# Turning batch 0's q and k in 64x64 pieces straight from their landed rows, with a new order on all engines

## The chip, the cores and the metric

The kernel runs on one core of a Trainium2 chip. The metric is the time of one execution in microseconds (us); lower is better. The kernel before took 135.5 us (the median of three runs, 134.92 to 135.55).

A core has engines that run side by side, each through its own list of instructions in order: PE (TensorE, matrix products and transposes, which write to PSUM), ACT (ScalarE) and DVE (VectorE), which work on SBUF and PSUM, POOL (GpSimd) and SP (SyncE), which here mostly issue DMA transfers. An engine that reaches an instruction whose inputs are not there waits, and all that stands behind it on that engine waits too.

## The reference

Two parts run one after the other, on 8 batches of 576 positions.

```python
# attention: q, k, v are (8 batches, 8 heads, 576, 64) in float32
scores = q @ k.transpose / 8 + bias       # bias = -slope[head] * |i - j|
mask   = (i - j >= 0) & (i - j < 128)     # each row sees itself and 127 before it
attn   = softmax(where(mask, scores, -1e9))
x      = (attn @ v), heads side by side   # (8, 576, 512)
# token mixing: w_q, w_k are (512, 64), w_out is (512, 512)
W      = (x @ w_q) @ (x @ w_k).T / 8      # (576, 576) for each batch
out    = relu(W @ x) @ w_out              # (8, 576, 512) in float32
```

As (x w_q) (x w_k)^T x is the same as (x w_q) ((x w_k)^T x), the kernel forms the small product G = (x w_k)^T x, 64 by 512, and never the 576 by 576 one.

## The kernel before, in words

The work is cut into some 730 named operations, each on one engine. Their order is written out by hand in `ORDER` (lines 35 to 118): one word for each, `name@engine`, for PE with `:bank` (the pair of PSUM banks, or one bank of it) and `+n`, which puts n filler matmuls (128x512, on a tile of zeros, `keep_busy`, line 299) ahead of the operation on PE. Each engine runs its words in this order. There is no planner in the kernel itself; semaphores follow from the data.

The stages of a batch b, with names as in `ORDER`:

- **Loads.** `Lq`, `Lk`, `Lv` fetch blocks n of 128 positions, 8 heads, and convert float32 to float16 on the way; `Lt` and `Lv b.4` fetch the last 64 positions of two batches together. All of them are issued by POOL (line 382), each as 128 KB that lands in SBUF. `Lw`, `Lwo` fetch the weights.
- **Turning.** `TQ` (and `TT` for the last 64 positions) transposes q and k on PE with an identity, `ETQ` and `ETT` copy the result from PSUM to `qkT` on ACT or DVE ("evict" it).
- **Scores.** `QK b.g.u`: scores of key block g, heads 4u to 4u+3. `EXP b.g.u` on ACT (line 555) takes the exponential; `MUL b.g` on DVE (line 565) multiplies by the exponential of bias and mask, which lies ready in `bias`, and in `biasl` for the last block.
- **Attention times v.** `PV` on PE; `R` and `X` on DVE divide by the row sums (line 619).
- **Token mixing.** `XT`, `EXT` turn x; `WQ`, `EWQ` and `WK`, `EWK` are the two projections; `G`, `EG` the small product; `MX` and `RM` the product with it and the relu; `OUT`, `EO`, `DO` the last projection, its eviction, and its transfer to memory. The `DO` of batches 0 to 5 stand on POOL behind all loads, those of 6 and 7 on SP.

Batch 0 starts differently, so that the first scores come early (`add_first`, line 390, and `add_tq0`, line 456). Its first 512 positions are loaded by heads: `Lf1.0` (k) and `Lf0.0` (q) fetch heads 0 to 3 as float32, issued by SP; `Lh0.1` (q) and `Lh1.1` (k) fetch heads 4 to 7 as float16, issued by POOL. Each partition p gets positions 4p to 4p+3 of four heads, head by head, in the tiles `nat2` and `nat3`, which batches 2 and 3 use later. Six operations `C` (line 409) then copy these rows into the tile of batch 0, with the four positions outermost and the heads inside, in float16: four with a cast (two each for k and q of heads 0 to 3; one on ACT, three on DVE), two without (heads 4 to 7, DVE). From there each `TQ0.u.j` (u: half of the heads, j: 0 for q, 1 for k) makes 16 transposes: 64 partitions by 128 columns (two heads side by side), so that a product fills all 128 output partitions. Two `ETQ0` for each `TQ0` evict it to `qkT0`, putting the positions back in order.

POOL builds the float32 identity `ident32` (`ident`); `idh` on DVE makes its float16 copy `identh`. `iota`, `dist`, `mask`, `bias0`, `bias1` make the bias tables, and `biasl0`, `biasl1` (line 353, two copies each) rearrange them for the last block. `zeros`, `empty`, `ones`, `pads`, `wqq` set constants and pads.

`cp` (line 234) is a plain copy on the engine named; `cpw` (line 240) is the same, but on ACT it copies pairs of float16 as one float32.

Of the kernel before, what the change touches and what calls it, by code (L numbers as in the profile page):

```python
# [50 lines left out]
EXP1.0.0@ACT WQ0.1@PE:30 Lq2.3@POOL EWK0@DVE EXP1.0.1@ACT XT1.2@PE:20 MUL1.1@DVE G0@PE:31 Lk2.2@POOL
EXT1.2@ACT TQ2.0@PE:0 EG0@ACT MUL1.0@DVE EWQ0.1@ACT Lt2.1@POOL PV1.3@PE:1 ETQ2.0@ACT MX0.0@PE:2
Lt2.0@POOL R1.3@DVE PV1.2@PE:3 RM0.0@ACT X1.3@DVE PV1.0@PE:0 Lwo3@POOL R1.2@DVE R1.0@DVE QK2.0.1@PE:1
X1.2@DVE Lwo0@POOL PV1.1@PE:2 EXP2.0.1@ACT X1.0@DVE Lwo2@POOL QK2.0.0@PE:3 Lwo1@POOL R1.1@DVE
EXP2.0.0@ACT MX0.1@PE:0 X1.1@DVE XT1.1@PE:1 Lk3.2@POOL RM0.1@DVE EXT1.1@ACT XT1.0@PE:2 TQ2.2@PE:3
Lk3.3@POOL EXT1.0@ACT WQ1.1@PE:10 ETQ2.2@ACT MUL2.0@DVE Lq3.2@POOL WK1@PE:11 QK2.1.0@PE:2 Lq3.3@POOL
EWK1@ACT MX0.4@PE:0 QK2.1.1@PE:3 EXP2.1.0@ACT RM0.4@DVE G1@PE:11 EWQ1.1@DVE Lq3.0@POOL TT2@PE:0
EXP2.1.1@ACT EG1@DVE QK2.2.0@PE:2 ETT2@DVE Lq3.1@POOL WQ1.0@PE:10 ETT3@ACT OUT0.2@PE:11 EWQ1.0@DVE
EXP2.2.0@ACT Lk3.1@POOL MUL2.1@DVE QK2.2.1@PE:3 EO0.2@ACT MX1.0@PE:0 Lv2.0@POOL QK2.3.1@PE:2
EXP2.2.1@ACT RM1.0@DVE OUT0.3@PE:10 Lk3.0@POOL EXP2.3.1@ACT OUT0.0@PE:11 MUL2.2@DVE Lv2.1@POOL  # L60
# [837 lines left out]
```

## Time and profile before

| | |
|---|---|
| time, median of 3 runs | 135.5 us (134.92 to 135.55) |
| the profiled execution's own time | 134.75 us |
| its span in the trace | 132.5 us |
| busy, of the span | PE 121.4 us, DVE 114.3, ACT 110.0, POOL 109.5 |
| moved by DMA | 25.12 MB, 190 GB/s in the mean |

The span runs from the first to the last instruction; 2.25 us of the execution's time lie around it. L12 is line 12 of the kernel; many operations go through helpers, so that all transposes show as L232, all other matmuls as L229, plain copies as L238 (DVE) and L236 (ACT), wide ones as L244 (DVE) and L242 (ACT). In a row of a timeline stand the start in us, the time it took (for several instructions, from the first start to the last end), the engine, line and operation, output and input, and the number of instructions; brackets give the engine's idle time before and what ended it. The chain of waits is the work that ended last, followed back from the end, at each step to what released it. In a table of stages each engine has its busy time and its instructions in brackets. Rows of DMA issues give the transfer, its size, and the time from issue to landing. PEld is the load of a matmul's stationary operand.

### The profile page before, as it was taken

Reading aid. Unit: us, or ns where it says so; the run is one execution under the profiler, and the core shown is the slowest. Engines: PE = TensorE matmul, PEld = TensorE weight load, DVE = VectorE, ACT = ScalarE, POOL = GpSimd, SP = SyncE. Lnnn points to the kernel's source line nnn. Section 1 sums busy time; section 2 is a strip of 40 time slices with the busy share of each in tenths; the row PEclk is TensorE's granted clock in tenths of the full one; section 3 lists DMA queues with packets and bytes.
Section 4 is the critical chain, followed back from the end, with each engine's and each line's share of the span. In section 5 each row is a group of like instructions: output and inputs, shape, how many; then the busy total and the mean of one; then the engine's idle time right before and its main releaser. Section 6 shows DMA issues by size and latency. Waiting matters only on the chain.

```text
span 132.5 us, 5417 instructions
## 1 busy us (share of the span) xinstructions
PE 121.4 (92%) x2346; PEld 77.8 (59%) x2346; DVE 114.3 (86%) x191; ACT 110.0 (83%) x161; POOL 109.5 (83%) x147
## 2 busy tenths in 40 slices
PE   6977798899889999999999999999999999999950
PEld 2324466667664577868567576677566756864520
DVE  6899799899959899999899999999899799975730
ACT  5728899999979899999899999999899889563330
POOL 7999979999799999999999999999977960980000
PEclk9999999999999999999999999999999999999996
DMA  3999999999999999999999999999999997598683
GB/s 113 291 159 153 157 153 160 152 143 143 175 159 151 153 154 153 155 149 154 157 153 154 158 149 155 154 157 153 155 172 397 396 378 238 148 308 331 241 306 96
DMA packets 110663, 25.12 MB, mean 190 GB/s; under 512 B 104816, under 2 KB 107888, under 8 KB 110640
## 3 DMA queue, kind: packets, MB, share of 16 engines
q0 software_dynamic: 108128, 21.37, 179.4%
q1 hardware_dynamic: 2512, 3.41, 7.5%
q8 instruction: 18, 0.29, 0.9%
q14 instruction: 5, 0.04, 0.1%
HBM read 29.62 MB, written 9.44 MB: 295 GB/s over the span
## 4 chain that ended last, share of the span: by engine, by line
PE 73%; DVE 15%; ACT 5%; issue 3%; POOL 0%; DVEq 0%; POOLq 0%; ACTq 0%
PE pair L229 63%; PE pair L232 10%; DVE pt L565 4%; ACT pt L555 3%; DVE nat L238 2%; DVE x L619 2%; DVE qkT L244 1%; DVE biasl L244 1%; DVE qkT L238 1%; ACT qkT L242 1%; DVE vtl L330 1%; DVE osb L238 0%; ACT qkT L236 0%; ACT osb L236 0%; DVE wint L317 0%
## 5 line engine op out<-in xcount | busy, mean ns | idle before, releaser
L555 ACT ACTIVATE pt<-pair 128x1024 f16<-128x1024 f32 x64 | 63.7, 1043 | 2.0 <-PE pair L229 1.6
L382 POOL DMA_DIRECT2D vt<-in_v_dram x32 | 32.4, 1136 | 0.0
L229 PE MATMUL pair<-wout_sb,rm 128*128 128x512 f16 (+1 forms) x132 | 32.1, 374 | 0.0
L382 POOL DMA_DIRECT2D nat<-in_q_dram x29 | 29.7, 1052 | 0.6 <-issue 0.5
L382 POOL DMA_DIRECT2D nat<-in_k_dram x29 | 28.7, 1056 | 0.3 <-DMA nat<-in_q_dram 0.3
L565 DVE TENSOR_TENSOR pt<-pt,bias 128x2048 f16<-128x2048 f16 x24 | 28.8, 1217 | 0.1
L229 PE MATMUL pair<-qkT 64*128 64x256 f16 (+2 forms) x320 | 23.4, 250 | 1.6 <-DVE qkT L244 0.7
L619 DVE TENSOR_TENSOR x<-pair,inv 128x512 f16<-128x512 f32 x32 | 21.7, 687 | 1.0
L229 PEld LDWEIGHTS <-pt 128*128 128x128 f16 (+1 forms) x576 | 18.4, 100 | 4.8 <-issue 2.3
L229 PE MATMUL pair<-vt,pt 128*128 128x65 f16 (+1 forms) x512 | 20.9, 194 | 0.0
L236 ACT COPY osb<-pair 128x512 f32<-128x512 f32 (+1 forms) x24 | 14.0, 594 | 5.7 <-PE pair L229 5.5
L229 PEld LDWEIGHTS <-rm 128*128 128x128 f16 x132 | 11.1, 97 | 11.1 <-issue 1.7
L229 PEld LDWEIGHTS <-qkT 64*128 64x128 f16 x320 | 11.4, 94 | 8.8 <-issue 3.9
L804 POOL DMA_DIRECT2D out_dram<-osb x24 | 13.6, 616 | 3.1 <-DVE osb L238 1.0
L232 PE MATMUL pair<-identh,nat 64*128 64x64 f16 x512 | 11.1, 192 | 1.6 <-DVE nat L238 0.9
L232 PEld LDWEIGHTS <-nat 64*128 64x128 f16 x512 | 9.3, 96 | 5.1 <-issue 1.6
L229 PE MATMUL pair<-fill 128*128 128x512 f16 x30 | 10.3, 478 | 1.8 <-DVE fill L362 1.2
L229 PE MATMUL pair<-xT,wqq_sb 128*128 128x256 f16 (+1 forms) x64 | 10.5, 287 | 0.2 <-ACT pt L555 0.2
L740 DVE TENSOR_SCALAR rm<-pair 128x1024 f16<-128x1024 f32 (+1 forms) x9 | 8.8, 983 | 1.8 <-PE pair L229 1.3
L242 ACT COPY qkT<-pair 128x1024 f32<-128x1024 f32 (+1 forms) x11 | 10.0, 907 | 0.2 <-PE pair L232 0.2
L738 ACT ACTIVATE rm<-pair 128x1024 f16<-128x1024 f32 x9 | 9.3, 1049 | 0.5 <-PE pair L229 0.5
L565 DVE TENSOR_TENSOR pt<-pt,biasl 128x2048 f16<-128x2048 f16 x8 | 9.7, 1215 | 0.0
(66 smaller groups left out, 168.1 us busy)
## 6 DMA issues: line engine op xcount, KB each, us to landing
out_dram<-osb POOLq DMA_DIRECT2D x24, 256.0 KB, 5.0
vt<-in_v_dram POOLq DMA_DIRECT2D x32, 128.0 KB, 5.8
nat<-in_q_dram POOLq DMA_DIRECT2D x28, 128.0 KB, 5.6
nat<-in_k_dram POOLq DMA_DIRECT2D x28, 128.0 KB, 5.7
out_dram<-osb SPq DMA_DIRECT2D x7, 256.0 KB, 2.1
out_dram<-osb POOLq DMA_DIRECT2D x6, 128.0 KB, 3.9
nat<-in_k_dram SPq DMA_DIRECT2D x1, 512.0 KB, 3.8
nat<-in_q_dram SPq DMA_DIRECT2D x1, 512.0 KB, 4.8
```

The costliest lines, as they stand in the source:

```text
L229: hold(nc.tensor.matmul(*a, **k))
L232: hold(nc.tensor.transpose(*a))
L236: hold(nc.scalar.copy(out_ap, in_ap))
L238: hold(nc.vector.tensor_copy(out=out_ap, in_=in_ap))
L242: hold(nc.scalar.copy(out_ap.bitcast(FP32), in_ap.bitcast(FP32)))
L382: op = add(kind, b, part, (eng,), deps, lambda o: q.dma_start(out=dst, in_=src), size=size)
L555: nc.scalar.activation(out=pt[:, u, 0:1024], in_=two(s.bank).rearrange("p e c -> p (e c)"), func=AF.Exp, scale=SCALE)
L565: nc.vector.tensor_tensor(out=pt[:, :, 0:1024], in0=pt[:, :, 0:1024], in1=bt, op=ALU.mult)
L619: nc.vector.tensor_tensor(out=x.rearrange("p (g h d) -> p g h d", g=2, h=4), in0=px(slice(0, 64)), in1=box["inv"].unsqueeze(3).broadcast_t ...
L738: hold(nc.scalar.activation(out=out_ap, in_=in_ap, func=AF.Relu, scale=WSCALE))
L740: hold(nc.vector.tensor_scalar(out=out_ap, in0=in_ap, scalar1=0.0, scalar2=WSCALE, op0=ALU.max, op1=ALU.mult))
L804: q.dma_start(out=out[b, P * st:P * st + P, c], in_=osb)
```

## The change

The `C` operations go. `first` now returns the landed rows themselves, in their own layout and type (float32 for heads 0 to 3, float16 for 4 to 7). `TQ0` turns pieces of 64 partitions by 64 columns, one head and one position of the four at a time: 32 pieces where there were 16. A piece of the upper or lower 64 partitions (`h`) of an even or odd head (`e`) goes to the PSUM bank h, partitions 64e to 64e+63. The float16 pieces are transposes with `identh`; the float32 ones are plain float32 matmuls with `ident32`, whose result is float32 in PSUM, so `ETQ0.0` casts to float16 as it evicts; `TQ0.0` needs `ident` and no longer `idh`. The loads `Lq2`, `Lk2`, `Lq3`, `Lk3` now wait for the `TQ0` that reads the tile they overwrite.

`ORDER` is new for all engines. Besides moves within an engine, 67 operations change between ACT and DVE, among them both `biasl`, `ETQ0.0.0.1`, `ETQ0.1.0.1`, `ETT1` (to ACT) and `ETQ0.0.1.1`, `ETQ0.1.1.1`, `EXT0.0` (to DVE). The fillers go from 30 to 22: 8 ahead of the first `TQ0` (10 before) and none ahead of the second (5 before). On DVE, `zeros` and `empty` now stand ahead of `dist` and `mask`, and `wqq` ahead of the first `ETQ0`. The loads of POOL are the same ones in a somewhat different order. The diff shows the start of both orders.

```diff
--- before.py
+++ after.py
@@ -33,88 +33,87 @@
 
 
 ORDER = """
-iota@POOL Lf1.0@SP pads@POOL Lf0.0@SP dist@DVE mask@DVE ident@POOL zeros@DVE bias0@ACT Lw0@POOL
-empty@DVE Lh1.1@POOL bias1@ACT ones@DVE idh@DVE Lh0.1@POOL Lt0.0@POOL C1.0.1@DVE C1.0.0@ACT biasl0@DVE
-Lt0.1@POOL TQ0.0.1@PE:0+10 biasl1@DVE ETQ0.0.1.1@ACT Lq1.3@POOL C0.0.0@DVE C0.0.1@DVE ETQ0.0.1.0@DVE
-Lk1.2@POOL TQ0.0.0@PE:1+5 ETQ0.0.0.0@ACT ETQ0.0.0.1@DVE Lk1.3@POOL QK0.0.0@PE:2+2 C1.1.0@DVE
-QK0.2.0@PE:3 EXP0.0.0@ACT QK0.1.0@PE:0 Lq1.2@POOL TQ0.1.1@PE:1 EXP0.2.0@ACT Lv0.1@POOL C0.1.0@DVE
-ETQ0.1.1.0@DVE TQ0.1.0@PE:2+1 Lv0.0@POOL ETQ0.1.1.1@ACT ETQ0.1.0.1@DVE EXP0.1.0@ACT ETQ0.1.0.0@DVE
-Lq1.0@POOL QK0.2.1@PE:3+3 QK0.1.1@PE:1 Lk1.1@POOL TT0@PE:0 EXP0.1.1@ACT QK0.0.1@PE:2 ETT0@DVE ETT1@DVE
-Lv0.2@POOL EXP0.0.1@ACT MUL0.1@DVE QK0.3.1@PE:1 Lk1.0@POOL EXP0.2.1@ACT MUL0.0@DVE Lq1.1@POOL
-EXP0.3.1@ACT TQ1.2@PE:0+7 Lv0.3@POOL MUL0.2@DVE QK0.3.0@PE:2 ETQ1.2@ACT PV0.0@PE:3 Lv1.3@POOL PV0.1@PE:1
-R0.0@DVE EXP0.3.0@ACT X0.0@DVE QK1.3.1@PE:0 Lv0.4@POOL R0.1@DVE QK1.2.1@PE:3 X0.1@DVE EXP1.3.1@ACT
-Lk2.1@POOL MUL0.3@DVE XT0.0@PE:2+1 QK1.3.0@PE:1 Lw1@POOL EXT0.0@ACT PV0.2@PE:0 Lk2.0@POOL EXP1.3.0@ACT
-QK1.2.0@PE:2 R0.2@DVE X0.2@DVE Lq2.1@POOL EXP1.2.1@ACT TQ1.0@PE:1 MUL1.3@DVE Lv1.2@POOL ETQ1.0@ACT
...
+pads@POOL Lf1.0@SP zeros@DVE iota@POOL empty@DVE Lf0.0@SP ident@POOL dist@DVE mask@DVE Lw0@POOL ones@DVE
+bias0@ACT Lh0.1@POOL bias1@ACT Lh1.1@POOL Lt0.0@POOL TQ0.0.1@PE:0+8 biasl1@ACT Lq1.3@POOL Lq1.2@POOL
+TQ0.0.0@PE:1 wqq@DVE Lt0.1@POOL ETQ0.0.1.0@DVE ETQ0.0.0.0@ACT Lk1.2@POOL ETQ0.0.0.1@ACT ETQ0.0.1.1@DVE
+QK0.0.0@PE:2+3 Lk1.3@POOL EXP0.0.0@ACT QK0.1.0@PE:3 idh@DVE TQ0.1.0@PE:1 Lv0.0@POOL biasl0@ACT
+TQ0.1.1@PE:0 ETQ0.1.0.0@DVE EXP0.1.0@ACT Lv0.1@POOL ETQ0.1.1.0@DVE ETQ0.1.0.1@ACT ETQ0.1.1.1@DVE
+QK0.0.1@PE:2+3 Lv0.2@POOL QK0.1.1@PE:3 EXP0.0.1@ACT QK0.2.0@PE:1 QK0.2.1@PE:0 Lq1.1@POOL EXP0.2.0@ACT
+MUL0.0@DVE Lq1.0@POOL EXP0.1.1@ACT TT0@PE:2+5 Lk1.1@POOL EXP0.2.1@ACT ETT0@DVE MUL0.1@DVE Lk1.0@POOL
+QK0.3.0@PE:1+1 ETT1@ACT EXP0.3.0@ACT TQ1.2@PE:3+1 Lv0.3@POOL MUL0.2@DVE QK0.3.1@PE:0 ETQ1.2@ACT
+PV0.1@PE:2 Lk2.1@POOL PV0.0@PE:1 EXP0.3.1@ACT R0.1@DVE QK1.3.0@PE:3 Lv0.4@POOL R0.0@DVE X0.0@DVE
+EXP1.3.0@ACT Lv1.3@POOL QK1.2.0@PE:0 X0.1@DVE QK1.3.1@PE:1 MUL0.3@DVE EXP1.3.1@ACT QK1.2.1@PE:2
+Lk2.0@POOL PV0.2@PE:3 Lq2.0@POOL R0.2@DVE EXP1.2.0@ACT X0.2@DVE TQ1.0@PE:1+1 Lq2.1@POOL MUL1.3@DVE
+XT0.0@PE:3 ETQ1.0@ACT PV0.3@PE:0 Lw1@POOL EXT0.0@DVE Lv1.2@POOL EXP1.2.1@ACT QK1.0.1@PE:1 R0.3@DVE
+QK1.1.0@PE:3 X0.3@DVE Lv1.0@POOL EXP1.1.0@ACT QK1.0.0@PE:2 MUL1.2@DVE XT0.1@PE:0 Lv1.1@POOL EXP1.0.0@ACT
...
@@ -283,7 +282,6 @@
             tc.add_to_no_dep_group(f"{group(op)}{op.eng}", i)
 
     columns = {
-        "C": lambda op: f"nat{op.batch}",
         "ETQ": lambda op: f"qkT{op.batch}",
         "ETT": lambda op: f"qkT{op.batch}",
         "QK": lambda op: f"qkT{op.batch}",
@@ -395,22 +393,14 @@
         if u == 0:
             raw = raw.bitcast(FP32)
             f = load("Lf", j, u, ("f", 512, 1024), [], raw.rearrange("p (h c) -> p h c", h=4), src, "SP")
-            parts = ((0, 2), (2, 4))
         else:
             raw = raw[:, 0:1024]
             f = load("Lh", j, u, ("c", 512, 1024), [], raw.rearrange("p (h c) -> p h c", h=4), src)
-            parts = ((0, 4),)
-        loads[0, j, u] = []
-        for i, (t0, t1) in enumerate(parts):
-            def cv(o, t0=t0, t1=t1):
-                (cpw if u else cp)(o.eng, first(j, u)[:, t0:t1],
-                                   raw.rearrange("p (h t d) -> p t h d", h=4, t=4)[:, t0:t1])
-
-            loads[0, j, u].append(add("C", j, f"{u}.{i}", EV, [f], cv))
+        loads[0, j, u] = [f]
 
     def first(j, u):
-        return nat_s[0][j].rearrange("p n h d -> p (n h d)").rearrange(
-            "p (u t h d) -> p u t h d", u=2, t=4, h=4)[:, u]
+        raw = nat_s[2 + u][j].rearrange("p n h d -> p (n h d)")
+        return (raw[:, 0:1024] if u else raw.bitcast(FP32)).rearrange("p (h t d) -> p h t d", h=4, t=4)
 
     def add_loads(b):
         pr = b // 2
@@ -421,7 +411,7 @@
         else:
             for n in range(4):
                 for j, t in enumerate((q, k)):
-                    loads[b, j, n] = load("L" + "qk"[j], b, n, ("c", 1024, 256), [tq.get((b - NNAT, j, n))],
+                    loads[b, j, n] = load("L" + "qk"[j], b, n, ("c", 1024, 256), [tq.get((b - NNAT, j, n)), *([tq[0, j, 2 * b - 4]] if b in (2, 3) else [])],
                                           nat_s[b % NNAT][j][:, n],
                                           t[b, :, P * n:P * n + P, :].transpose([1, 0, 2]))
         for t in range(4):
@@ -453,21 +443,29 @@
         r = slice(64 * h, 64 * h + 64)
         tp(out_ap, in_ap, identh[r, r])
 
+    def turned(bank, u):
+        return (two(bank).bitcast(F16)[:, :, 0:512] if u else two(bank)).rearrange("p h (a q) -> p h a q", q=64)
+
     def add_tq0(u, j):
         def em(o):
             for c in range(2):
                 for t in range(4):
-                    for h in range(2):
-                        src = first(j, u)[64 * h:64 * h + 64, t, 2 * c:2 * c + 2, :].rearrange("p a b -> p (a b)")
-                        flip(halves(o.bank, 8, 1)[:, h, 4 * c + t, 0, :], src, h)
-
-        t = add("TQ", 0, f"{u}.{j}", PE, [*loads[0, j, u], idh], em, banks=2, mode=1)
+                    for e in range(2):
+                        for h in range(2):
+                            r = slice(64 * h, 64 * h + 64)
+                            dst = turned(o.bank, u)[64 * e:64 * e + 64, h, 4 * c + t, :]
+                            if u:
+                                tp(dst, first(j, u)[r, 2 * c + e, t, :], identh[r, r])
+                            else:
+                                mm(dst, first(j, u)[r, 2 * c + e, t, :], ident32[r, r], start=True, stop=True)
+
+        t = add("TQ", 0, f"{u}.{j}", PE, [*loads[0, j, u], idh if u else ident], em, banks=2, mode=3)
         for n in (2 * u, 2 * u + 1):
             tq[0, j, n] = t
         for h in range(2):
             def ev(o, h=h):
                 dst = qkT_s[0][:, j, 2 * u:2 * u + 2, 256 * h:256 * h + 256].rearrange("p c (q t) -> p c q t", t=4)
-                src = halves(t.bank, 8, 1)[:, h, :, 0, :].rearrange("p (c t) q -> p c q t", c=2)
+                src = turned(t.bank, u)[:, h].rearrange("p (c t) q -> p c q t", c=2)
                 cp(o.eng, dst, src)
 
             evt[0, j, u, h] = add("ETQ", 0, f"{u}.{j}.{h}", EV, [t], ev, frees=[t], half=h, size=0)
```

More of the change, by code (lines that the diff above doesn't have):

```diff
@@ L51 @@
[L51 to L60, printed above, removed]
-OUT0.1@PE:00 EO0.0@ACT Lv3.3@POOL EO0.3@DVE MX1.4@PE:3 QK2.3.0@PE:2 EO0.1@ACT Lv2.2@POOL RM1.4@DVE
-TQ3.2@PE:1 EXP2.3.0@ACT MX1.1@PE:3 ETQ3.2@DVE OUT1.1@PE:01 Lv2.3@POOL RM1.1@ACT OUT1.4@PE:00 Lk4.0@POOL
@@ new lines @@
+EXP1.1.1@ACT MUL1.0@DVE XT1.2@PE:01 XT0.2@PE:30 Lk2.2@POOL TQ2.0@PE:1 EXT0.2@ACT EWQ0.0@ACT EXT1.2@DVE
+WK0@PE:31 ETQ2.0@ACT MUL1.1@DVE Lk2.3@POOL PV1.3@PE:2 Lwo0@POOL QK2.0.1@PE:0 R1.3@DVE PV1.0@PE:1
+X1.3@DVE EXP2.0.1@ACT Lt2.0@POOL WQ0.1@PE:30 R1.0@DVE PV1.1@PE:2 X1.0@DVE Lwo1@POOL EWK0@ACT EWQ0.1@ACT
+QK2.0.0@PE:0 Lwo2@POOL R1.1@DVE PV1.2@PE:1 X1.1@DVE EXP2.0.0@ACT Lwo3@POOL G0@PE:31 R1.2@DVE Lt2.1@POOL
+X1.2@DVE XT1.0@PE:2 EG0@ACT Lq3.3@POOL EXT1.0@DVE MX0.4@PE:0 MX0.1@PE:1 RM0.4@ACT XT1.1@PE:3 RM0.1@ACT
@@ new lines @@
+MX0.0@PE:2 Lq3.2@POOL EXT1.1@DVE TQ2.2@PE:0 RM0.0@DVE WQ1.0@PE:30 ETQ2.2@ACT Lk3.2@POOL WK1@PE:31
+Lk3.3@POOL QK2.2.1@PE:1 EWK1@DVE QK2.2.0@PE:2 EXP2.2.1@ACT QK2.1.1@PE:0 EWQ1.0@DVE Lk3.0@POOL G1@PE:31
+MUL2.0@DVE EXP2.1.1@ACT WQ1.1@PE:30 Lv2.0@POOL EG1@DVE OUT0.2@PE:10 EXP2.2.0@ACT EWQ1.1@DVE Lq3.1@POOL
+MX1.1@PE:0 EO0.2@ACT QK2.1.0@PE:3 Lk3.1@POOL RM1.1@DVE TT2@PE:2 OUT0.0@PE:11 ETT3@ACT ETT2@ACT
+Lq3.0@POOL EXP2.1.0@ACT MUL2.2@DVE QK2.3.0@PE:2 MX1.4@PE:0 Lv2.1@POOL OUT0.1@PE:10 EXP2.3.0@ACT
@@ L118 @@
+OUT7.1@PE:00 EO7.2@ACT DO7.2@SP OUT7.4@PE:01 EO7.1@DVE DO7.1@SP EO7.4@ACT DO7.4@SP
 """
```

115 lines of the change are left out of this document (57 added, 58 removed).

## The prediction

> **What bounds the kernel now.** I read the busy times of the page first (they stand in the table above; no engine is far ahead of the others), then a table of four stages, then the chain of waits at the start, then single loads against the operations that use them.
>
> ```profile
> 10.50:28.40 17.90, 15.14 (x352) 10.21 (x349) 15.94 (x27) 17.36 (x21) 16.90 (x21) 1.00 2.37 154
> 28.40:66.40 38.00, 36.80 (x797) 25.11 (x796) 34.78 (x56) 35.02 (x49) 36.86 (x45) 1.00 2.28 154
> 66.40:102.00 35.60, 35.52 (x759) 23.37 (x754) 34.02 (x53) 34.82 (x50) 33.93 (x43) 1.00 2.35 174
> 102.00:128.00 26.00, 25.84 (x400) 15.91 (x395) 20.82 (x39) 16.80 (x32) 12.00 (x23) 1.00 0.83 292
> ```
>
> The columns after the length are PE, PEld, DVE, ACT and POOL. From 10.5 to 28.4 ACT is the full engine (17.36 of 17.90 us) and PE has 2.8 us free. From 28.4 on PE is the full one: 1.2 us free up to 66.4, 0.1 up to 102, 0.2 up to 128. ACT keeps 3.0 us free in the second stage and 0.8 in the third. So nothing after 66.4 can be won by a change at the start unless everything arrives there earlier.
>
> What holds ACT back at the start is in the chain of waits:
>
> ```profile
> 5.19 0.45 DVE nat L238
> 5.64 1.69 DVE biasl L244 x4
> 7.33 1.70 DVE nat L238 x2
> ...
> 9.46 0.59 ACT qkT L236
> ...
> 10.10 0.41 PE pair L229 x4
> ...
> 10.53 1.03 ACT pt L555
> ```
>
> DVE casts half of k, copies `biasl`, casts q (`C0.0.0`, `C0.0.1`); only then can `TQ0.0.0` turn q, ACT evict it, `QK0.0.0` run, and ACT's stream of exponentials begin at 10.53.
>
> Second, the loads, which POOL issues one behind the other:
>
> ```profile
> 15.61 1.02 POOL L382 DMA_DIRECT2D vt<-in_v_dram  x1
> vt<-in_v_dram POOLq DMA_DIRECT2D x1, 128.0 KB, 7.5
> 23.07 0.69 PE L229 MATMUL pair<-vt,pt 128*128 128x65 f16 x16
> 28.62 0.92 POOL L382 DMA_DIRECT2D nat<-in_k_dram  x1
> nat<-in_k_dram POOLq DMA_DIRECT2D x1, 128.0 KB, 6.0
> 34.57 0.66 PE L232 MATMUL pair<-identh,nat 64*128 64x64 f16 x32
> 75.87 1.26 POOL L382 DMA_DIRECT2D nat<-in_k_dram  x1
> nat<-in_k_dram POOLq DMA_DIRECT2D x1, 128.0 KB, 5.8
> 82.39 0.63 PE L232 MATMUL pair<-identh,nat 64*128 64x64 f16 x32
> 18.24 0.82 POOL L382 DMA_DIRECT2D vtl<-in_v_dram  x1 [0.73 <-DMA vt<-in_v_dram]
> ```
>
> The load issued at 15.61 lands 7.5 us later, at 23.1, and `PV0.3` uses it at 23.07: no slack. The one at 28.62 lands at 34.6, and `TQ2.2` starts at 34.57: no slack. The one at 75.87 lands at 81.7 and `TQ6.0` starts at 82.39: 0.7 us. In the new order the last load that `PV0.3` needs is still the 17th of POOL's loads, and that of `TQ2.2` the 31st, as before. So the loads are a second bound, which the change moves only as far as POOL's own idle time shrinks (0.73 us in the last row, where POOL waits for an earlier load to land).
>
> **The change part by part.** The durations are of the profiled execution, 134.75 us, of which 132.5 are span.
>
> Removed: the six `C`, and `biasl` from DVE.
>
> ```profile
> 10.13 1.51 DVE L244 COPY nat<-nat 128x1024 f16<-128x1024 f16 x2
> L242 ACT COPY xT<-pair 128x512 f32<-128x512 f32 x7 | 4.1, 590 | 0.5 <-PE pair L232 0.5
> L242 ACT COPY xT<-pair 128x128 f32<-128x128 f32 x5 | 1.3, 268 | 0.2 <-PE pair L232 0.2
> L242 ACT COPY qkT<-pair 128x256 f32<-128x256 f32 x2 | 0.8, 375 | 0.2 <-PE pair L232 0.2
> ```
>
> DVE loses 0.45 + 1.70 + 1.51 us of `C` and 1.69 of `biasl`, 5.4 in all, most of it on the path to 10.53. ACT loses one cast, ahead of that path, and gets `biasl`: per half a copy of 384 float32 and one of 128; between the rows for 512 (0.59) and 128 (0.27) the first is 0.48, so 0.75 per half. `biasl1` stands ahead of the first eviction, `biasl0` behind the first exponential.
>
> The new turning, `TQ0.0`:
>
> ```profile
> 1.25 0.50 SPq L382 DMA_DIRECT2D nat<-in_q_dram  x1
> nat<-in_k_dram SPq DMA_DIRECT2D x1, 512.0 KB, 3.8
> nat<-in_q_dram SPq DMA_DIRECT2D x1, 512.0 KB, 4.8
> 1.19 4.45 PE L229 MATMUL pair<-fill 128*128 128x512 f16 x10 [1.19 <-DVE fill L362]
> 5.77 0.61 PE L232 MATMUL pair<-identh,nat 64*128 64x64 f16 x16
> 6.31 1.63 PE L229 MATMUL pair<-fill 128*128 128x512 f16 x5
> 17.24 0.64 PE L232 MATMUL pair<-identh,nat 64*128 64x64 f16 x32
> 0.74 0.45 SPq L382 DMA_DIRECT2D nat<-in_k_dram  x1
> ```
>
> k lands at 0.74 + 3.8 = 4.55, q at 1.25 + 4.8 = 6.05. Ten fillers take 4.45 us, so eight end near 4.6, and `TQ0.0.1` can start at 4.65 instead of 5.77. Sixteen transposes take 0.61 us there, of which about 0.24 is the latency of the last: eight pairs (the two halves of the partitions run side by side) at 0.049 us a pair. At 17.24 thirty-two take 0.64, less 0.19 for the last: 0.029 a pair, since PE is faster by then; the five fillers from 6.31 take 1.63, between the slow and the fast step, so the turn lies near 7.1.
>
> No float32 matmul is in the trace. Lower end: four pieces at a time (their output halves differ as well) at the pair's price: 8 x 0.049 = 0.4 us for an operation. Upper end: each piece alone with its whole latency: 32 x 0.24 = 7.6. I take 1.6: 16 pairs at 0.049, twice that for twice the bytes of each element; it stays near the row of the same shape. By it `TQ0.0.1` runs from 4.65 to 6.2, and `TQ0.0.0` starts there (q landed at 6.05), does 57% until 7.1 and the rest at the fast price (0.93 x 0.43 = 0.4): 7.5, with the last latency 7.7. What the section TensorE Precision Notes of the page FP8 and Floating Point Precision in the Trainium skill says, that true float32 takes four passes through the array, would with pairs give 3.1 an operation instead of 1.6, and the first exponential at 10.75; no run here shows it. TensorEngine Tiling (Trainium skill, section Tile-to-Partition Mapping) has four independent 64x64 tiles, which would bring that back to 1.6; its section Restrictions adds that column tiling switches the fast weight load off, which speaks against the change.
>
> Evictions from float32: ACT's 0.59 for 512 float32 is the same as the 0.59 for float16 in the chain, so nothing. ACT evicts both halves of q (7.7 to 8.3, 8.9) while `QK0.0.0` runs (0.41), and `EXP0.0.0` starts at **8.9 instead of 10.53: 1.6 us earlier**. Ahead of it on ACT are the bias tables, which come later now:
>
> ```profile
> 2.61 0.55 DVE L334 MEMSET qkT<- 128x256 uint32 x2
> 3.42 0.94 DVE L330 MEMSET vtl<- 64x1056 uint32 x1 [0.26 <-issue]
> 2.65 2.56 ACT L348 ACTIVATE bias<-wint 128x256 f16<-128x256 f32 x8 [0.63 <-DVE wint L317]
> ```
>
> `zeros` and `empty` (1.49) go ahead of `mask`, so the tables run from 4.15 to 6.7 and `biasl1` to 7.45. That hides behind `TQ0.0.0` with 0.25 us to spare; if PE were faster it would cost that. On DVE `wqq` waits for `Lw0` ahead of the first evictions of k; those must be done by 8.3 and have 2 us from 6.2.
>
> What ACT does with the 1.6 us. Before, seven exponentials and one eviction filled 10.53 to 17.92 (`ETQ1.2`):
>
> ```profile
> 17.92 1.01 ACT L242 COPY qkT<-pair 128x1024 f32<-128x1024 f32 x1
> 15.27 2.36 DVE L565 TENSOR_TENSOR pt<-pt,bias 128x2048 f16<-128x2048 f16 x2
> 3.70 0.78 POOL L382 DMA_DIRECT2D nat<-in_q_dram  x1
> nat<-in_q_dram POOLq DMA_DIRECT2D x1, 256.0 KB, 6.0
> ```
>
> Now the same seven and one stand there with `biasl0` (0.75) and `ETT1` (0.38): 8.9 + 7.39 + 1.13 = 17.4, half a microsecond ahead; `EXT0.0` then leaves ACT for DVE (0.59), so 1.1 ahead. DVE gains more: heads 4 to 7 land by 3.70 + 6.0 = 9.7, are turned by 10.4 and evicted by 11.1 to 11.8, and the first `MUL` can start when ACT has done `EXP0.0.1`, near 13.4 instead of 15.27.
>
> The eight fillers fewer (0.22 each) and the longer `TQ0.1` (32 pieces, 0.5 to 1.0 us for 0.41) lie where PE has 2.8 us free: nothing. The loads that now wait for `TQ0` stand on POOL at the place of the load issued at 18.24 and behind it, 10 us after `TQ0.0` ends: nothing.
>
> The sum: 1.1 us on ACT and 1.9 on DVE by 18 us. Then the loads of `PV0.3` and `TQ2.2`, with no slack, stop PE at the same places. If the stream of loads does not move, an earlier ACT and DVE can only fill PE's 1.2 us of idle time between 28.4 and 66.4; if it moves by POOL's 0.73, that much gets through at these two places and the rest has to come from PE's idle time; at `TQ6.0` there are 0.7 us of slack. I take **0.8**, two thirds of PE's 1.2 and about as much as the slack at `TQ6.0`: 134.75 - 0.8 = 133.95 for an execution like the profiled one. The median of the three runs is 0.75 above that execution, so 134.7 for the median.
>
> **The rivals.**
>
> - *The loads swallow it.* `TQ2.2` waits for the same 31st load, POOL's idle time stays, and PE's idle time behind it belongs to other waits. For it: two zero slacks. Against it: ACT and DVE are both ahead. Gain 0 to 0.4: 135.3.
> - *The float32 pieces cost twice what I take, 3.1 us an operation on slow PE.* Then `TQ0.0.1` does 2.45 / 3.1 of its work by 7.1 and ends at 7.5, `TQ0.0.0` at 9.55, and the first exponential starts at 10.75, 0.2 late; DVE is still ahead by what `biasl` and `C` took, so no more than 0.1 comes of it: 135.4. For it: no operation here works on pieces that are halves both ways, so that four at once is not shown. Against it: pairs overlap in every row of transposes. This is the time by the four passes of the Trainium skill's page FP8 and Floating Point Precision (TensorE Precision Notes) without the four tiles of its page TensorEngine Tiling.
> - *Slower: they cost more than that.* The 3.1 us are the point from which it decides. At 6.2 (one piece at a time, and 16 pairs' worth twice over) `TQ0.0.1` ends at 9.3, `TQ0.0.0` at 13.2, and the first exponential starts at 14.4, 3.9 us late, on an engine that is 97% busy until 28.4. Of the 3.9, ACT's 3.0 us of idle time between 28.4 and 66.4 may give back 2.0: 134.75 + 1.9 = 136.65, or 137.4 for the median. For it: the upper end of 7.6 lies beyond it. Against it: again the pairs.
> - *The new order brings waits of its own.* 67 operations change between ACT and DVE; one wait on PE behind a late ACT in stages where PE has 0.1 us free is paid in full. A price of one eviction or exponential (0.6 to 1.0): 136.3. Against it: DVE, 34.0 of 35.6 us busy from 66.4 on, has 5.4 us less behind it when it gets there.
>
> **How the numbers follow.** The forecast has 0.43, the loads 0.23, pieces at twice the price 0.11, dear pieces 0.10, waits of the new order 0.13. What a measurement can tell from no change is about 0.5%, 0.68 us. Faster by that: 0.36 of the forecast's 0.43, 0.05 of the loads' and 0.02 of the rest: 0.43. Slower: all 0.10 of the dear pieces, 0.07 of the waits, 0.02 each of the loads and of the double price: 0.21. Within: 0.36. The forecast alone is 133.9 (all 1.6 get through) to 135.1. The range reaches below it by POOL's 0.73 us, and above over the waits and part of the dear pieces: 133.2 to 136.8.
>
> **What would show it.** Right: float32 matmuls with `ident32` of 1.6 us for 32 or less, the first exponential before 9.5, the first `MUL` before 14, POOL's wait near 18 shorter, PE's idle time between 28 and 66 under 0.6 us. Wrong: pieces of 3 us or more; a start 1.5 us earlier with `TQ2.2` again at 34.6; or ACT, not PE, on the chain between 30 and 100.

## The result, and the profile after

The changed kernel took **133.57 us** (median of 21 runs, 133.09 to 135.33), the kernel before 134.58 us (21 runs beside them, 133.80 to 136.18): 0.9926 of its time, with a 95% interval of 0.9902 to 0.9949. That is 1.0 us faster. Some executions of the kernel before and of several others run 1 to 5 per cent longer than the rest; ratios leave these out, medians don't. The profiled execution of the changed kernel took 134.83 us (span 132.9), 1.3 us more than its median, while that of the kernel before (134.75, span 132.5) lies near its own. Two single executions therefore don't show the gain, and their stretches have to be read against the scatter. Of an execution's time 2.16 to 2.30 us lie outside the span in every execution of the kernel before that ran beside the kernels of this document, and 1.84 to 1.94 in all 21 of the changed kernel. That is 0.33 us in the mean, a third of the gain, which no row of a timeline can show; what it comes from, no run here tells.

The start of PE in the timeline of the changed kernel:

```profile
5.01 2.48 PE L228 MATMUL pair<-ident,nat 64*64 64x64 f32 x128 [0.22 <-DMA nat<-in_k_dram]
...
9.01 0.45 PE L231 MATMUL pair<-identh,nat 64*64 64x64 f16 x32
9.70 0.45 PE L231 MATMUL pair<-identh,nat 64*64 64x64 f16 x32 [0.24 <-DMA nat<-in_k_dram]
...
12.97 0.61 PE L228 MATMUL pair<-qkT 64*128 64x256 f16 x7 [0.78 <-issue]
...
17.50 0.87 PE L228 MATMUL pair<-vt,pt 128*128 128x65 f16 x23 [0.22 <-DMA vt<-in_v_dram]
...
34.26 0.65 PE L231 MATMUL pair<-identh,nat 64*128 64x64 f16 x32
```

Both fp32 `TQ0.0` stand in the first row: 64 pieces show as 128 matmuls, two for each, and take 2.48 us together. The f16 ones take 0.45 us each. In the fourth row PE stops 0.78 us in the middle of `QK0.2.0` with no releaser but its own issue; in the fifth `PV0.1` waits for batch 0's v rows (its first matmul stands at 17.07, ahead of the wait). `TQ2.2` starts at 34.26 (34.57 before). ACT in the same stretch:

```profile
8.63 1.02 ACT L553 ACTIVATE pt<-pair 128x1024 f16<-128x1024 f32 x1
9.55 0.70 ACT L241 COPY biasl<-bias 128x384 f32<-128x384 f32 x2
...
13.40 2.86 ACT L553 ACTIVATE pt<-pair 128x1024 f16<-128x1024 f32 x3 [0.82 <-PE pair L228]
...
17.29 1.06 ACT L241 COPY qkT<-pair 128x1024 f32<-128x1024 f32 x1
```

The first exponential starts at 8.63 instead of 10.53, 1.90 us earlier; `ETQ1.2` at 17.29 instead of 17.92, 0.63 earlier. Of what is lost on the way, 0.82 is ACT's wait for the stalled PE. The first `MUL` starts at 12.61 instead of 15.27. The stages, POOL's wait, and the chain of waits up to 18 us:

```profile
10.50:28.40 17.90, 14.57 (x331) 9.59 (x330) 14.91 (x23) 16.75 (x22) 16.74 (x20) 1.00 2.40 156
28.40:66.40 38.00, 36.42 (x766) 24.36 (x765) 34.01 (x57) 33.76 (x47) 37.11 (x46) 1.00 2.30 155
66.40:102.00 35.60, 35.36 (x773) 23.84 (x768) 34.55 (x50) 34.88 (x52) 34.43 (x44) 1.00 2.29 176
102.00:128.00 26.00, 26.00 (x402) 15.97 (x400) 19.61 (x36) 17.99 (x35) 11.27 (x21) 1.00 0.81 286
```

```profile
13.26 1.76 POOL L380 DMA_DIRECT2D nat<-in_q_dram  x2 [1.16 <-DMA nat<-in_q_dram]
```

```profile
9.49 0.78 POOL vt L380
10.26 7.19 DMA vt<-in_v_dram
17.45 0.04 issue
17.50 0.63 PE pair L228 x15
```

ACT now has 1.2 us free up to 28.4 (0.5 before). POOL's wait for a landed load has not shrunk: it is 1.16 us at 13.26 where it was 0.73 at 18.24. The chain of the start no longer goes through DVE's casts but through POOL's loads and the transfer that lands at 17.45.

### The profile page after: what moved, and what is told of

It is laid out like the page before. It is cut to its first block, busy times and chain, and to the rows that moved or that the text cites. A ratio compares the mean times of both kernels' runs of the same rounds, so it can differ in the third digit from the quotient of the medians.

```text
span 132.9 us, 5633 instructions
## 1 busy us (share of the span) xinstructions
PE 121.3 (91%) x2466; PEld 78.3 (59%) x2466; DVE 109.6 (82%) x177; ACT 111.5 (84%) x169; POOL 109.4 (82%) x147
## 4 chain that ended last, share of the span: by engine, by line
PE 64%; ACT 11%; POOL 7%; DVE 6%; DMA 5%; issue 4%; POOLq 0%; DVEq 0%; ACTq 0%
PE pair L228 58%; ACT pt L553 7%; PE pair L231 6%; DMA vt<-in_v_dram 5%; POOL nat L380 4%; DVE x L617 3%; POOL natt L380 1%; ACT osb L235 1%; ACT qkT L241 1%; DVE inv L614 1%; DVE pt L563 1%; ACT xT L241 1%; POOL vt L380 1%; POOL wq_sb L380 0%; DVE xT L243 0%
## 5 line engine op out<-in xcount | busy, mean ns | idle before, releaser
L380 POOL DMA_DIRECT2D vt<-in_v_dram x32 | 31.5, 1122 | 0.0
L380 POOL DMA_DIRECT2D nat<-in_k_dram x29 | 29.9, 1060 | 0.9 <-DMA natt<-in_q_dram 0.8
L228 PE MATMUL pair<-vt,pt 128*128 128x65 f16 (+1 forms) x512 | 21.5, 194 | 0.6 <-DMA vt<-in_v_dram 0.2
L228 PEld LDWEIGHTS <-rm 128*128 128x128 f16 x132 | 11.0, 97 | 10.8 <-issue 1.5
L241 ACT COPY qkT<-pair 128x1024 f32<-128x1024 f32 (+1 forms) x15 | 11.5, 774 | 0.4 <-PE pair L231 0.2
L237 DVE COPY osb<-pair 128x512 f32<-128x512 f32 x13 | 8.9, 686 | 3.4 <-PE pair L228 2.1
L736 ACT ACTIVATE rm<-pair 128x1024 f16<-128x1024 f32 (+1 forms) x10 | 10.1, 1036 | 0.6 <-PE pair L228 0.6
L228 PE MATMUL pair<-xT,wqq_sb 128*128 128x256 f16 (+1 forms) x64 | 10.5, 287 | 0.0
L231 PE MATMUL pair<-identh,nat 64*128 64x64 f16 (+1 forms) x512 | 10.2, 191 | 0.2 <-DMA nat<-in_k_dram 0.2
L231 PEld LDWEIGHTS <-nat 64*128 64x128 f16 (+1 forms) x512 | 8.8, 96 | 1.9 <-issue 1.4
L614 DVE RECIPROCAL inv<-pair 128x8 f32<-128x8 f32 x36 | 7.4, 205 | 2.6 <-PE pair L228 2.2
```

The costliest lines, as they stand in the source:

```text
L228: hold(nc.tensor.matmul(*a, **k))
L231: hold(nc.tensor.transpose(*a))
L237: hold(nc.vector.tensor_copy(out=out_ap, in_=in_ap))
L241: hold(nc.scalar.copy(out_ap.bitcast(FP32), in_ap.bitcast(FP32)))
L380: op = add(kind, b, part, (eng,), deps, lambda o: q.dma_start(out=dst, in_=src), size=size)
L614: nc.vector.reciprocal(out=box["inv"], in_=px(64))
```

## The experiments

Three theories at first. L: the stream of loads holds the kernel from 17 to 34 us, and the start's lead dies there. S: the lead passes on to the end. O: the new order packs the later stages better. Times are medians in us of all executions; a ratio is to the kernel before, which ran beside each set on the same chip (the column "before there"). The experiments ran in sets on three chips, and the changed kernel itself did not run beside the last two sets (from before_twice on), so kernels of different sets are compared by their ratios. `PV0.1` stands with its first matmul, which can come shortly before its wait.

| run | time (runs) | before there | ratio, interval | first EXP | `PV0.1` | `TQ2.2` | span profiled |
|---|---|---|---|---|---|---|---|
| before | 134.58 (21) | | | 10.53 | 18.33 | 34.57 | 132.5 |
| after | 133.57 (21) | 134.58 | 0.9926, 0.9902 to 0.9949 | 8.63 | 17.07 | 34.26 | 132.9 |
| after_again | 133.86 (10) | 134.66 | 0.9931, 0.9900 to 0.9962 | 9.17 | 17.21 | 34.24 | 132.5 |
| turn_only | 133.88 (9) | 134.66 | 0.9937, 0.9902 to 0.9972 | 10.06 | 17.97 | 34.24 | 131.9 |
| order_only | 133.91 (11) | 134.66 | 0.9948, 0.9919 to 0.9976 | 9.16 | 17.94 | 34.74 | 132.5 |
| pads_dve | 134.32 (12) | 134.66 | 0.9969, 0.9941 to 0.9997 | 8.44 | 18.53 | 35.33 | 132.6 |
| after_no_v1 | 133.36 (12) | 134.34 | 0.9918, 0.9880 to 0.9955 | 8.63 | 16.85 | 33.95 | 130.9 |
| before_no_v1 | 133.88 (12) | 134.34 | 0.9951, 0.9928 to 0.9975 | 9.99 | 17.76 | 34.03 | 132.1 |
| late_start | 134.04 (12) | 134.34 | 0.9992, 0.9958 to 1.0025 | 9.65 | 17.20 | 34.19 | 131.7 |
| late_w | 134.03 (6) | 134.13 | 0.9986, 0.9948 to 1.0025 | 8.43 | 16.82 | 34.48 | 132.1 |
| few_fill | 133.77 (6) | 134.13 | 0.9962, 0.9921 to 1.0002 | 8.58 | 17.55 | 34.35 | 131.9 |
| both | 134.30 (6) | 134.13 | 0.9999, 0.9958 to 1.0041 | 8.44 | 17.72 | 34.73 | 132.4 |
| one_tile | 135.88, 137.04 (2 of 4) | 134.13 | 1.0172, 1.0099 to 1.0246 | 12.27 | 19.98 | 36.99 | 134.0 |

**The changed kernel again, and its two halves.** after_again is the changed kernel unchanged. turn_only has its code with the order of before, less the `C`; order_only has the code of before with the new order, and the six `C` put back in:

```diff
 turn_only, ORDER
-... Lt0.0@POOL C1.0.1@DVE C1.0.0@ACT biasl0@DVE Lt0.1@POOL TQ0.0.1@PE:0+10 ...
+... Lt0.0@POOL biasl0@DVE Lt0.1@POOL TQ0.0.1@PE:0+10 ...
 order_only, ORDER
-... ones@DVE bias0@ACT Lh0.1@POOL bias1@ACT ...
+... ones@DVE idh@DVE C1.0.1@DVE C0.0.0@DVE C0.0.1@DVE bias0@ACT Lh0.1@POOL C1.0.0@ACT bias1@ACT ...
```

> The changed kernel once more, beside the others of this set and with a second profile. Ratio to the kernel before 0.990 to 0.995 by every theory. In the trace: the float32 pieces again at 1.1 to 1.2 us for the 32 of one operation, the first exponential between 8.5 and 9.5 us, and, if the loads hold the kernel (theory L), the uses of loads between 17 and 34 us again within 0.4 us of their landing.

> The new turning alone: the code of the changed kernel with the order of the kernel before, less the six C. biasl stays on DVE, idh ahead of it. Theory L (the loads hold the kernel between 17 and 34 us, the start's lead dies there): the first exponential comes at 9 to 9.5 us instead of 10.5, but the loads stand in the old order, so 0 to 0.4 us are gained: ratio 0.997 to 1.000. Theory S (the lead of the start passes to the end): 1.0 to 1.5 us, ratio 0.989 to 0.993. Theory O (the new order packs the later stages better, and the turning hardly matters): ratio 0.998 to 1.002.

> The new order alone: the code of the kernel before, with the six C put into the new order (k's two casts ahead of its turning, q's two on DVE behind them, the two copies of heads 4 to 7 on DVE behind the evictions of k). Theory L: the new order by itself has the same loads at the same ranks, the first exponential comes at about 10 us, and what the changed kernel gains from being early is gone: ratio 0.996 to 1.000. Theory S: ratio 0.998 to 1.003, as nothing is earlier. Theory O: nearly the whole gain, ratio 0.991 to 0.995.

By the ratios turning alone gives 0.85 us (0.4 to 1.3 by its interval), the order alone 0.7 (0.3 to 1.1), both together 0.9 to 1.0. So the halves don't seem to add, though their intervals would still allow it. None of the three theories meets both runs: order_only comes out as O had it, turn_only does not, and L's and S's ranges miss order_only (its interval reaches into L's). S's premise for it, that nothing is earlier, was wrong as well: its first exponential came at 9.16, though PE ran at half clock from 7.82 to 14.65; turn_only's, at 10.06, came later than L's 9 to 9.5. Nor does the first exponential of a profile tell the time: turn_only, 0.47 us ahead of the kernel before, gains 0.85, while late_w, both and pads_dve, 2.1 us ahead, gain 0.2, 0 and 0.4.

In after_again the first exponential is 0.54 us later than in the other profile of the same kernel, because PE's clock came to full speed only near 6.9 us (5.2 there), and at `TQ1.0` and `TQ2.0` the two are 0.13 and 0.00 us apart: half a microsecond of start is gone by 27 us. Its `TQ0.0` row beside the one above:

```profile
5.17 2.87 PE L228 MATMUL pair<-ident,nat 64*64 64x64 f32 x128 [0.38 <-DMA nat<-in_k_dram]
```

**Loads issued earlier: pads_dve.** Two memsets move from POOL to DVE, so POOL reaches its first load 0.5 us sooner.

```diff
-pads@POOL Lf1.0@SP zeros@DVE iota@POOL ... ones@DVE
+Lf1.0@SP zeros@DVE iota@POOL ... ones@DVE pads@DVE
```

> The changed kernel with the two memsets of pads moved from POOL, where they stand ahead of all loads for 0.56 us, to DVE behind ones, where DVE waits anyway. The stream of loads then starts 0.56 us earlier and nothing else changes. Theory L: 0.3 to 0.56 us faster than the changed kernel, ratio to the kernel before 0.988 to 0.991. Theories S and O: no change against the changed kernel, ratio 0.991 to 0.994.

That failed. The table of DMA issues has 7.2 us for the v load issued at 10.26 in the changed kernel and 7.5 for the one issued at 9.96 here, so both land near 17.45; by its 13th load POOL has given the lead back (13.20, against 13.26 in the changed kernel):

```profile
13.20 1.75 POOL L380 DMA_DIRECT2D nat<-in_q_dram  x2 [1.33 <-DMA nat<-in_q_dram]
```

POOL's pace does not set the landings, the transfers do (155 GB/s from 10.5 to 28.4 us here, 156 in the changed kernel, 154 before). pads_dve came out slower than the changed kernel by its ratio, with an interval that overlaps; its profile shows why it could. PE's clock fell to half for one stretch, 14.15 to 17.56. In a window table the last three numbers of a row are the granted clock (1.00 is full), the DMA share and GB/s:

```profile
14.00:15.00 1.00, 1.00 (x4) 0.37 (x3) 0.00 (x0) 1.00 (x2) 1.00 (x3) 0.57 2.43 155
15.00:16.00 1.00, 1.00 (x18) 0.38 (x16) 0.00 (x0) 1.00 (x2) 1.00 (x2) 0.50 2.46 170
16.00:17.00 1.00, 1.00 (x17) 0.47 (x13) 0.72 (x2) 0.74 (x2) 1.00 (x2) 0.50 2.34 146
```

`ETQ1.2` comes at 18.41 there instead of 17.29, and `TQ2.2` at 35.33.

**The kernel before, profiled twice** (before_twice, unchanged).

> The kernel before, unchanged, profiled a second time. In its first profile the 11th load landed at 17.94 us and the 31st at 34.66; in the four profiles of changed kernels the 11th landed between 16.7 and 17.5 and the 31st between 33.88 and 34.13. If the late landings belong to the old order, they come again (31st after 34.4); if they are the scatter of one execution, the 31st lands near 34.0 here too, and the loads then set the same end for both kernels. Expected: near 34.1 us.

The 31st load did not land near 34.1: it landed at 34.7 again, and `TQ2.2` started at 34.79, so the late landings are no accident of one execution. They are not the order of the loads either: turn_only has that order too, and its 31st load landed at 34.0. What makes them late is open. With 34.57 and 34.79 before, and 34.26 and 34.24 after, the change is 0.3 to 0.55 us ahead at 34 us.

**Four loads fewer: after_no_v1 and before_no_v1.**

```diff
         for t in range(4):
+            if b == 1:
+                loads[b, "v", t] = loads[0, "v", t]
+                continue
             loads[b, "v", t] = load(
```

> The changed kernel without the four loads of batch 1's v rows (Lv1.0 to Lv1.3); batch 1 multiplies by batch 0's v rows instead, so batch 1's result is left wrong in its values, with the same instructions on PE, ACT and DVE. Four of the 31 loads that PE waits for up to TQ2.2 are gone, and those behind them come earlier. Theory L (the stream of loads holds the kernel between 17 and 34 us): 1.0 to 2.0 us faster than the changed kernel, about 132.0 us, with TQ2.2 before 33.3 us in the profile. Theory S (PE's and ACT's own work holds it, the start's lead passes on to the end): the same as the changed kernel within 0.3 us.

> The kernel before with the same four loads left out, and batch 1 on batch 0's v rows. L: the old start gains as well by the loads, but it then has its own later start to pay, so the distance to the changed kernel without these loads grows from 1.0 us to 1.6 us or more (the first exponential is 1.9 us later in it); about 133.7 us. S: as the kernel before, and the distance stays 1.0 us.

By the ratios the changed kernel gains about 0.1 us by it (0.9918 against 0.9926 and 0.9931), as S had it, and the kernel before 0.65. The distance between the two is 0.45 us here, neither L's 1.6 nor S's 1.0, though its error of about 0.6 still takes in 1.0. L in its strong form falls: `TQ2.2` comes at 33.95 instead of 34.26, while its load had landed at 30.23, 3.7 us before. From `PV0.1` to `TQ2.2` PE needs 17.1 us without the four loads and 17.2 with them. So PE gets to `TQ2.2` by itself hardly before the load lands, and taking loads away frees little. What remains of L is a single place at 17 us, the load that `PV0.1` waits for, and one near the end, below.

**A later start: late_start.**

```diff
-            for c, n in ((0, 192), (192, 64)):
+            for c, n in ((0, 192), (192, 64)) * (3 if u else 1):
```

> The changed kernel with the copies of biasl1 written three times on ACT, which is about 1.4 us more ahead of ACT's first eviction; nothing else is changed. L: the start's lead over the loads is lost but little else, 0 to 0.5 us slower than the changed kernel. S: 1.2 to 1.5 us slower.

The first exponential starts at 9.65, 1.02 us later than in the changed kernel. In the timeline of late_start:

```profile
6.75 1.94 ACT L241 COPY biasl<-bias 128x384 f32<-128x384 f32 x6
...
9.65 1.02 ACT L553 ACTIVATE pt<-pair 128x1024 f16<-128x1024 f32 x1
...
12.55 3.79 ACT L553 ACTIVATE pt<-pair 128x1024 f16<-128x1024 f32 x4
...
17.20 0.91 PE L228 MATMUL pair<-vt,pt 128*128 128x65 f16 x24
17.34 1.09 ACT L241 COPY qkT<-pair 128x1024 f32<-128x1024 f32 x1
```

ACT does not wait near 13 us (0.82 in the changed kernel), `ETQ1.2` is 0.05 us later and `PV0.1` finds its load there. So **in this one execution the microsecond given back was slack**, which in the changed kernel PE's stall and the load at 17.45 eat. The times don't bear that out: by the ratios late_start is 0.9 us slower than the changed kernel (0.9992 against 0.9926; the intervals allow 0.3 to 1.4), between L's and S's expectation. Inside the span its median is that of the kernel before beside it (132.1 both). The profiled execution, at 133.57, was among the fastest of its twelve (133.54 to 135.72), and its load landed at 17.12 instead of 17.45. Whether the lead is slack or is paid in most executions stays open.

**The load and the stall, one by one: late_w, few_fill, both.**

```diff
 late_w
-... mask@DVE Lw0@POOL ones@DVE ... TQ0.0.0@PE:1 wqq@DVE Lt0.1@POOL ...
+... mask@DVE ones@DVE ... TQ0.0.0@PE:1 Lt0.1@POOL ...
-... Lv0.4@POOL R0.0@DVE ... X0.3@DVE Lv1.0@POOL
+... Lv0.4@POOL Lw0@POOL R0.0@DVE ... X0.3@DVE wqq@DVE Lv1.0@POOL
 few_fill
-TQ0.0.1@PE:0+8 ... QK0.0.0@PE:2+3 ... QK0.0.1@PE:2+3
+TQ0.0.1@PE:0+7 ... QK0.0.0@PE:2 ... QK0.0.1@PE:2
```

> The changed kernel with the load of wq (the first one that POOL issues) moved behind batch 0's last v load, and wqq, the op that reads it, moved on DVE behind X0.3; nothing is left out. Ten loads instead of eleven of that size stand ahead of batch 0's v rows. Theory G (one gate: the start's lead dies at PV0.1, which waits for batch 0's v rows at 17.45 us, and behind it PE's and ACT's own work sets the time): these rows land 0.8 us earlier, near 16.6 us, PV0.1 doesn't wait, and the kernel is 0.2 to 0.6 us faster than the changed one. Rival W (PE's and ACT's work is as late at 17 us as the load): PV0.1 stays near 17.1 us, and the time within 0.2 us.

> The changed kernel with seven of its filler matmuls left out (the three ahead of QK0.0.0, the three ahead of QK0.0.1, one of the eight ahead of TQ0.0.1), which is 14 instructions fewer on PE's queue ahead of QK0.2.0. If the stall near 13 us belongs to a place in PE's instruction queue (the 446th recorded instruction, as in the four earlier kernels with the new turning), it stands 14 instructions further in the work, behind QK0.2.0 and near QK0.2.1's end, and ACT's idle 0.82 us ahead of EXP0.2.0 is gone. If it belongs to that product (a wait for a bank, or for ACT), it stays at QK0.2.0. Time: G says within 0.2 us of the changed kernel, since the gate at 17.45 us stays; W says 0.3 to 0.7 us faster. A third way: the clock, without these fillers at half rate for a stretch, 0.5 to 1 us slower.

> late_w and few_fill in one kernel: the load of wq later, and the fillers left out. G and the stall together: PV0.1 at 16.6 us or earlier, 0.5 to 1.0 us faster than the changed kernel; if each alone does nothing and both do, the load and PE's stall end at one time. W, or the clock: no faster than few_fill.

late_w does not decide between G and W: the v rows land only 0.27 us earlier (17.18), not 0.8, and `PV0.1` still waits for them.

```profile
12.71 0.61 PE L228 MATMUL pair<-qkT 64*128 64x256 f16 x7 [0.72 <-issue]
...
17.23 0.87 PE L228 MATMUL pair<-vt,pt 128*128 128x65 f16 x23 [0.21 <-DMA vt<-in_v_dram]
```

My 0.8 took wq for a load like the others; it is 64 KB in 128 rows, against 128 KB in 1024 pieces of 128 bytes. By `TQ2.0` (27.71 against 27.43) what it won is lost, since the load now stands ahead of batch 1's. By its ratio late_w is 0.8 us slower than the changed kernel, which neither G nor W had. few_fill decides on the stall. Its timeline, where the stall used to be:

```profile
11.65 1.47 PE L228 MATMUL pair<-qkT 64*128 64x256 f16 x12 [0.23 <-ACT qkT L235]
...
12.73 2.85 ACT L553 ACTIVATE pt<-pair 128x1024 f16<-128x1024 f32 x3 [0.20 <-PE pair L228]
...
13.16 0.13 PEld L228 LDWEIGHTS <-fill 128*128 128x128 f16 x2 [0.53 <-issue]
```

All of `QK0.2` now runs through, ACT's wait is down to 0.20, and the break stands ahead of a filler. Counted from the start it is the 224th weight load in the changed kernel and in few_fill, and in turn_only, after_again, pads_dve, after_no_v1, late_w and `both` too (in late_start PE waits for ACT just ahead of it); which work stands at that place differs. So **the stall belongs to a place in PE's instruction queue**. The trace has transfers of 16 KB on a DMA queue of kind "instruction". In these eight profiles the first after the start begins at 10.3 to 10.8 us, and PE goes on 2.3 to 2.5 us after that in every one of them (10.64 and 12.97 in the changed kernel, 10.81 and 13.16 in few_fill). Where PE came to the place later than that it did not stop: 2.75 us after the transfer's start in late_start, 3.4 in one_tile. Before and order_only, which have 256 matmuls and loads fewer by then, have that transfer at 15.9 and 14.6 us, and no such stall. The later breaks fit as well: PE goes on at 36.91 and 56.99 in the changed kernel, 2.4 and 2.3 us after such a transfer began; in after_again, where the transfer for the first of these places began two microseconds sooner, there is no break. So the stall is most likely the wait for this transfer. No run moved the transfer by itself, so that last step is argued, not shown. few_fill's clock paid for the missing fillers, as its third way had it (0.76 in the mean of this stretch):

```profile
10.50:17.50 7.00, 6.00 (x87) 3.12 (x87) 4.17 (x6) 6.22 (x9) 6.00 (x7) 0.76 2.42 157
```

so its time (0.9962) and its `PV0.1`, at 17.55, say nothing of what the stall costs. `both` ends no better: the load has landed at 17.30 and no longer holds `PV0.1`; PE, at half clock from 12.67 to 16.08, gets there at 17.72.

**Four quarters at once? one_tile.** The same pieces, eight in a row through one 64x64 quarter of the array.

```diff
-            for c in range(2):
-                for t in range(4):
-                    for e in range(2):
-                        for h in range(2):
-                            r = slice(64 * h, 64 * h + 64)
+            for e in range(2):
+                for h in range(2):
+                    r = slice(64 * h, 64 * h + 64)
+                    for c in range(2):
+                        for t in range(4):
```

> The changed kernel with the 32 pieces of each TQ0 op in another order: eight pieces in a row go through the same 64x64 quarter of the array, instead of four pieces through four quarters in turn; the same pieces, the same results. In the changed kernel's trace groups of four start within 20 ns, 58 ns behind the group before, 1.2 us for 32 fp32 pieces. If four pieces run at once in four quarters, a row of eight in one quarter costs more: over 2.0 us for 32 fp32 pieces, and over 0.8 us for 32 f16 ones (now 0.45). If the pace is that of issue, both stay. By G some 1.7 us more on TQ0.0 costs the time under 0.5 us, by W some 1.2 us.

```profile
4.75 6.39 PE L228 MATMUL pair<-ident,nat 64*64 64x64 f32 x128
...
12.63 1.51 PE L231 MATMUL pair<-identh,nat 64*64 64x64 f16 x64
...
36.99 0.65 PE L231 MATMUL pair<-identh,nat 64*128 64x64 f16 x32
```

3.2 us an fp32 operation instead of 1.24, 0.75 an f16 one instead of 0.45: pieces in different quarters run at once. The first exponential comes at 12.27, 3.6 us late, `TQ2.2` at 36.99, 2.7 late. The profiled execution took 135.88 us, 2.3 over the changed kernel's median; the ratio to the kernel before, from two executions, is 2.5 per cent (3.3 us) above the changed kernel's. So 2.3 to 3.3 of the 3.6 us are paid, more than G or W had for the 1.7 they counted on.

**Near the end.** after_again has none of the later stalls and gets to batch 6's v rows before they have landed. Its second stage, and the row of `PV6.1` in its timeline:

```profile
28.40:66.40 38.00, 37.91 (x794) 25.24 (x793) 35.39 (x58) 35.10 (x50) 37.24 (x46) 1.00 2.34 156
```

```profile
99.05 0.66 PE L228 MATMUL pair<-vt,pt 128*128 128x65 f16 x16 [1.12 <-DMA vt<-in_v_dram]
```

PE has 0.09 us free from 28.4 to 66.4 (1.58 in the other profile) and then waits 1.12 us for the 105th of POOL's 108 loads. `PV6.1` starts within 0.3 us of that landing in late_start, late_w, few_fill and both too: in five of the nine profiles of the new order with all its loads. From `PV6.1` to the end each of the nine needs 33.4 to 33.7 us, so where PE gets there that early, this landing sets the end. after_no_v1, whose stream is four loads shorter, does not wait and ends 1.6 us sooner (130.9 of span against 132.5); but its ratio is only 0.1 us better, so how often that wait holds an unprofiled run stays open.

## Why the prediction was right, and where it was not

- **Direction: right. Size: right by luck.** Forecast a gain of 0.8, measured 1.0 (0.7 to 1.3 by the interval of the ratio). But the 0.8 was to come out of PE's 1.2 us of idle time between 28 and 66 us, and it does not lie there. Most of that idle time was one stop of PE, which waited neither for ACT nor for DVE:

```profile
37.00 0.38 PE L229 MATMUL pair<-wk_sb,xT 128*128 128x64 f16 x7 [0.74 <-issue]
```

  An earlier ACT or DVE cannot fill it, and the changed kernel has such stops too (below). What the runs show of the gain is 0.3 to 0.55 us by `TQ2.2`, before that stretch, and 0.33 outside the span, which no term of the sum had; the 0.1 to 0.4 left is within the scatter.
- **The time itself: 134.7 forecast, 133.57 measured,** below the 133.9 to 135.1 that the forecast alone allowed. Of the 1.1 too much, 0.9 is one term: I put the median 0.75 above the profiled execution, from three runs with a median of 135.5. Over 21 runs the kernel before has 134.58, 0.17 below it.
- **Price of the fp32 pieces: right, by two errors that cancel.** I took 1.6 us on slow PE. The pair was 2.48 us with PE at full clock from 5.2, and 2.87 with 1.72 of it for the first where the clock came at 6.9. I had it from 16 pairs at twice the price of f16; the trace has eight groups of four, each at about four times the f16 price (3.2 against 0.75 us for 32 pieces in one_tile), which makes the same product. That ratio agrees with the four passes that the Trainium skill names (FP8 and Floating Point Precision, TensorE Precision Notes), and the quarters with the four independent tiles of its page TensorEngine Tiling (Tile-to-Partition Mapping), though they bring 2.6 times the pace, not four. The rivals with double price and dear pieces are out; one_tile shows what the latter would have cost, 2.3 us or more over the changed kernel.
- **The path to the first exponential: right, 8.63 for 8.9.** The bias tables ran from 4.16 to 6.72, `biasl1` to 7.45, and PE ended `TQ0.0.0` at 7.49.
- **ACT at `ETQ1.2`: right in the sum, wrong in the terms.** 17.29 for 17.4. The lead at the start was larger (1.90), and 0.82 of it went into a PE stall that no step of mine had.
- **"The longer `TQ0.1` ... nothing": the step that failed in kind.** I costed the instructions' time and not their number. The 256 more bring PE to a break in its queue ahead of ACT's work. In the profiled execution it is nearly free, because the load at 17.45 holds `PV0.1` anyway.
- **POOL's 0.73: wrong.** I let the stream move by that much. Earlier issues land at the same time (pads_dve); the 31st load did land 0.75 us earlier (33.92 for 34.67), while the wait, which I had named as a sign to get shorter, grew to 1.16.
- **The zero slacks of `PV0.3` and `TQ2.2`: right as coincidence, wrong as a cause.** `TQ2.2` came 0.3 to 0.55 us earlier, and after_no_v1 shows that PE gets there no more than 0.3 us sooner with its load landed long before. My own sign of being wrong, a start 1.5 us earlier with `TQ2.2` again at 34.6, came close: 1.9 earlier, and 34.26.
- **PE's idle time between 28 and 66 under 0.6: 1.58 in one profile, 0.09 in the other.** The difference is PE stopping inside one operation, as at `WK1`:

```profile
35.34 0.72 PE L228 MATMUL pair<-wk_sb,xT 128*128 128x64 f16 x19
36.91 0.20 PE L228 MATMUL pair<-wk_sb,xT 128*128 128x64 f16 x1 [0.85 <-issue]
```

  where after_again has the same twenty in one row:

```profile
35.33 0.75 PE L228 MATMUL pair<-wk_sb,xT 128*128 128x64 f16 x20
```

- **Waits of the new order:** none found. From `TQ2.2` to the last transfer's issue the kernel before took 93.9 us and the changed kernel 94.65; less PE's breaks with no releaser in that stretch (0.74, and 0.85 + 0.64) it is 93.2 for both. So in these two executions the new order behind 34 us loses nothing to waits of its own, and gains nothing either.

**Open.** The profiles place 0.3 to 0.55 us of the gain at `TQ2.2`, and 0.33 us lies outside the span, of unknown cause; the rest is not located. Why each half of the change seems to give three quarters of it is not settled either. About 0.25 us of what each half gains lies outside the span. That inside it both end at the same places (the load at 17.45, PE's own 17 us behind it) fits, and no run takes all of that away at once.
